# A new order for the loading phase of a fused attention and gated feed-forward kernel, with x of batch 0 loaded as fp32 and every batch's x read by column-tiled matmuls

## The chip, the cores and the metric

The kernel runs on one core of a Trainium2 chip. A core has a matmul engine (TensorE; its matmuls are PE in the profile, its weight loads PEld), a vector engine (VectorE, DVE), a scalar engine for activations (ScalarE, ACT), a general engine (GpSimd, POOL) and an engine that issues transfers (SyncE, SP). Each has its own instruction queue, executed in order. They meet through semaphores, in a large on-chip memory (SBUF) and in the accumulators of the matmul engine (PSUM). [...]

The metric is the device time of one execution in microseconds. Before the change three runs gave a median of 223.96 us (223.51 to 224.49).

## The reference

There are 8 batches with 8 heads each. A batch has 512 tokens x and 32 state rows, of width 64 per head.

```python
scores = scale * x @ state.T          # (512, 32) per head
a = softmax(scores)                   # over the 32 state rows
xread = a @ state                     # (512, 64)
scores2 = scale * state @ x.T         # the same scores, transposed
a2 = softmax(scores2)                 # over the 512 tokens
sread = a2 @ x                        # (32, 64)
x = concatenate([xread, sread], axis=2)   # heads side by side: 544 rows of 512 per batch
gate = 1 / (1 + exp(-(x @ w_gate)))   # (rows, 1536)
out = (gate * (x @ w_val)) @ w_out    # (rows, 512)
```

In all, 4352 rows of 512 numbers are written. All inputs and the output are fp32.

## The kernel before

Matmuls run in bf16. For the rows that come from tokens, a @ state @ w is computed as a @ (state @ w): `sw_visit` and `sw_wide` multiply the state of a batch with column ranges of `wg` and `wv` and leave the products in PSUM, `sw_cp` copies them to the tile `SW`, and `gv_mm(b, f)` multiplies `SW` with the transposed a (`aT`) for the 128 columns of slice f. `gv_th` (ACT) and `gv_glu` (DVE) form the gated product; the sigmoid is a tanh, with the factor 0.5 put on the output. `out_mm(b, k)` multiplies four slices with `wo`; the output of one row group is complete after three such calls, is copied by ACT and sent out.

For a, `xT_mm` and `xT_cp` (or transposing DMAs on SP, `at_xT_dma`) transpose x, `S_mm` makes scores, `S_exp` exponentials, `n_sum` or `n_sums` and `n_mul` or `n_muls` normalise over the state rows, and `aT_mm` with `aT_cp` (or transposing DMAs, `aT_dma`) transposes the result. `at_Eb` makes a bf16 copy of the exponentials on POOL.

The second softmax needs, for each state row, a sum over tokens of exponential times x (the read of x) and the sum of the exponentials. Before the change there are two ways. For batches 0 to 2, `sr_mm` makes 16 matmuls with x as the stationary side (L265), and the sums either with eight matmuls against `ones` (batch 0, L262) or with one matmul of sums that POOL has folded (`p_tok`, `p_fold`, `n_add`; L257); `sr_fin` divides (L270, L278) into the tile `XS`. For batches 3 to 7, `rd_mm` makes 32 column-tiled matmuls (L292): 32 columns of exponentials are the stationary side, so that four of them use four quarters of the array; the moving side is a copy of x with a column of ones (`xs`, made by `cast_xs`), so that the sum comes as column 65. `rd_fin` divides and `rd_dma` transposes into `XS` by a DMA on SP. `XS` is used for the 256 state rows at the end.

The order of the work is written out by hand: each engine executes its instructions in the order of the calls. PSUM has four pools: `GV` with two banks, `OU` and `AT` with one, `SWP` with four. Batches 0 and 1 are computed call by call (L477 to L731), together with all loads of weights; from L734 a loop goes over batches 2 to 8, where 8 stands for the state rows, with one slice of batch b, one part of the output of b - 1 and some preparation of b + 1 in each step.

Loads in the first phase: x of batch 0 comes half as fp32 on SP with casts on three engines (L478, L491, `cast_xp`) and half by POOL's queue with conversion (`load_xh`, L483); x of batch 1 and all weights come by POOL's queue (`load_xh`, `load_w`, `load_wo`), and so does the state of batches 2 to 7 (`load_sb`). POOL issues a load when it reaches it, behind its own work. `warm(n, place)` issues n matmuls of 512 columns whose result is not read.

Of the kernel before, what the change touches and what calls it, by code (L numbers as in the profile page):

```python
# [8 lines left out]
FP = mybir.dt.float32  # L9
# [7 lines left out]
def kernel(  # L17
# [36 lines left out]
    ones = wp.tile((128, 2, 128), BF, name="ones")  # L54
# [130 lines left out]
    def n_add(b):  # L185

        E2 = ap_.tile((128, 2, 2, 4, Ns), FP, name="E2", bufs=1)
        held["E4", b] = ap_.tile((128, 2, 4, Ns), FP, name="E4")
        nc.vector.tensor_tensor(E2, E1s[b][:, 0:2], E1s[b][:, 2:4], ALU.add)
        nc.vector.tensor_tensor(held["E4", b], E2[:, 0], E2[:, 1], ALU.add)  # L190

    def p_fold(b):

        E4, add = held["E4", b].rearrange("p e j n -> p e (j n)"), nc.gpsimd.tensor_tensor
        F, G = (ap_.tile((128, 2, 4 * Ns), FP, name=n, bufs=1) for n in ("F", "G"))
        half = [slice(e * 64, e * 64 + 64) for e in range(2)]
        for e in range(2):
            pool(F[half[e], 0], E4[half[1 - e], e])
        for e in range(2):
            add(G[half[e], 0], E4[half[e], e], F[half[e], 0], ALU.add)  # L200
        for q in range(4):
            r = q ^ 1
            pool(F[32 * q:32 * q + 32, 1], G[32 * r:32 * r + 32, 0])
        add(G[:, 1], G[:, 0], F[:, 1], ALU.add)
        hl = held["hl", b] = ap_.tile((128, 4 * Ns), BF, name="hl")
        pool(hl, G[:, 1])
        for e in range(2):
            lo = slice(e * 64 + 32, e * 64 + 64)
            add(hl[lo], G[lo, 1], hl[lo], ALU.subtract)

    def p_tok(b):

        add = nc.gpsimd.tensor_tensor
        E5 = ap_.tile((128, 2, 4, Ns), FP, name="P1", bufs=1)
        E4 = held["E4", b] = ap_.tile((128, 2, 4, Ns), FP, name="E4")
        add(E4, E1s[b][:, 0], E1s[b][:, 1], ALU.add)
        add(E5, E1s[b][:, 2], E1s[b][:, 3], ALU.add)
        add(E4, E4, E5, ALU.add)

# [27 lines left out]
    def sr_parts(b):  # L247
        ps = held["sr", b]
        return (ps[:, 0:256].rearrange("p (j e n) -> p j e n", j=4, e=2),
                ps[:, 256:384].rearrange("p (j n) -> p j n", j=4))  # L250

    def sr_mm(b, place):
        Eb = Ebs[b]
        held["sr", b] = place[0].tile((128, 512), FP, name="srp", tag=place[1])
        sr, sm = sr_parts(b)
        if ("hl", b) in held:
            nc.tensor.matmul(sm, pick, held["hl", b], start=True, stop=True)  # L257
            terms = []
        else:
            terms = [(e, Eb[:, c, e]) for e in range(2) for c in range(4)]  # L260
        for i, (e, rhs) in enumerate(terms):
            nc.tensor.matmul(sm, ones[:, e], rhs, start=(i == 0), stop=(i == len(terms) - 1))  # L262
        for j in range(4):
            for c in range(4):
                nc.tensor.matmul(sr[:, j], xbs[b][:, c, 2 * j:2 * j + 2].rearrange("p h d -> p (h d)"),  # L265
                                 Eb[:, c, :, j], start=(c == 0), stop=(c == 3))

    def sr_inv(b):
        r2 = held["r2", b] = ap_.tile((128, 4, Ns), FP, name="r2")
        nc.vector.reciprocal(r2, sr_parts(b)[1])  # L270

    def sr_fin(b):
        if ("r2", b) not in held:
            sr_inv(b)
        sr, r2 = sr_parts(b)[0], held["r2", b]
        for e in range(2):
            rows = slice(e * 64, (e + 1) * 64)
            nc.vector.tensor_tensor(XS[rows, b], sr[rows, :, e], r2[rows], ALU.mult)  # L278

# [3 lines left out]
    def rd_mm(b):  # L285

        ps = AT[0].tile((128, 512), FP, name="rdp", tag=AT[1])
        rd = held["rd", b] = ps[:, :2 * D + 2].rearrange("p (e d) -> p e d", e=2)
        for e in range(2):
            for c in range(4):  # L290
                for j in range(4):
                    nc.tensor.matmul(rd[j * Ns:(j + 1) * Ns, e], Ebs[b][:, c, e, j], xs[:, c, 2 * j + e, :D + 1],  # L292
                                     start=(c == 0), stop=(c == 3))

    def rd_fin(b):
        rd = held["rd", b]
        r2 = ap_.tile((128, 2, 1), FP, name="rr")
        nc.vector.reciprocal(r2, rd[:, :, D:])
        xr = held["xr", b] = ap_.tile((128, 2, D), BF, name="xr")
        nc.vector.tensor_tensor(xr, rd[:, :, :D], r2.to_broadcast((128, 2, D)), ALU.mult)  # L300
# [84 lines left out]
    def out_mm(b, k, place=None):  # L385
# [10 lines left out]
        if f0 == 8:  # L396
            res = fp.tile((128, 512), FP, name="res", bufs=4)
            nc.scalar.activation(res, ops[b, c], AF.Copy, scale=0.5)  # L398
            if b < B:
                n = 256 if 4 * (B - 1) - 4 <= 4 * b + c < 4 * (B - 1) else 512  # L400
# [25 lines left out]
    def warm(n, place):  # L426

        ps = place[0].tile((128, 512), FP, name="warm", tag=place[1])
        for _ in range(n):
            nc.tensor.matmul(ps.rearrange("p (r k) -> p r k", r=4), ones[:, 0], ones[:, 0].unsqueeze(1).to_broadcast((128, 4, 128)), start=True, stop=True)  # L430
# [44 lines left out]
    pick = wp.tile((128, 128), BF, name="pick")  # L475
    pre = wp.tile((128, 2), FP, name="pre")
    make_identity(nc, ident)  # L477
    load_xp(0, nc.sync, 0, 2)  # L478
    for e in range(2):
        nc.vector.memset(ones[:, e, e * 64:e * 64 + 64], 1.0)  # L480
        nc.vector.memset(ones[:, e, 64 - e * 64:128 - e * 64], 0.0)
    warm(1, SWP)
    load_xh(0, 4, 4)  # L483
    warm(2, GV)
    warm(2, AT)
    load_s(0, nc.scalar)
    cast_s(0, vec)
    load_xh(1, 4, 4)
    warm(2, GV)
    warm(4, SWP)  # L490
    load_xp(0, nc.sync, 2, 2)  # L491
    cast_xp(0, act, 2, 2)
    zero(sbz, vec)
    sT_mm(0, SWP)
    xT_mm(0, 1, SWP)
    cast_xp(0, pool, 0, 2)
    cast_x(0, vec, 0, 2)
    zero(sTd, vec)
    xT_mm(0, 0, SWP)
    sT_pad(1, vec)  # L500
    xT_cp(0, 0, act)
    sT_pad(0, act)
    xT_mm(0, 3, SWP)
    S_mm(0, 0, SWP, (0,))
    load_xh(1, 0, 4)
    xT_mm(0, 2, GV)
    load_sb(1)
    xT_cp(0, 1, vec)
    S_mm(0, 0, AT, (1,))
    load_w(1, 256, 256)  # L510
    S_exp(0, 0)
    cast_x(0, vec, 6, 2)
    xT_mm(1, 2, SWP, 2)
    xT_cp(0, 2, vec)
    xT_cp(0, 3, act)
    S_mm(0, 1, GV, (0,))
    S_mm(0, 1, AT, (1,))
    warm(1, GV)
    n_sum(0, 0)
    S_exp(0, 1)  # L520
    cast_x(0, act, 2, 2)
    load_w(0, 256, 256)
    xT_mm(1, 0, GV, 2)
    xT_cp(1, 0, act, 2)
    load_w(0, 1024, 512)
    xT_cp(1, 2, vec, 2)
    S_mm(1, 1, OU)
    S_mm(1, 0, SWP)
    n_sum(0, 1)
    load_w(1, 1024, 512)  # L530
    sT_mm(1, SWP)
    n_mul(0, 1, vec)
    S_exp(1, 1)
    cast_x(0, vec, 4, 2)
    n_mul(0, 0, pool)
    at_Eb(0)
    aT_mm(0, AT)
    S_exp(1, 0)
    load_w(1, 0, 256)
    sT_cp(1, act)  # L540
    sw_visit(0, 256, 256)
    sr_mm(0, OU)
    sw_visit(1, 256, 256)
    n_sums(1)
    n_muls(1, vec)
    load_w(0, 0, 256)
    aT_cp(0, 0, act)
    sw_cp(0, 256, 2, 0, act)
    sw_cp(0, 256, 2, 1, act)
    aT_cp(0, 1, act)  # L550
    gv_mm(0, 2, GV)
    load_sb(2)
    sw_cp(1, 256, 2, 1, vec)
    gv_th(0, 2)
    sw_cp(1, 256, 2, 0, act)
    aT_mm(1, AT)
    gv_glu(0, 2)
    aT_cp(1, None, act)
    sw_visit(1, 1024, 512, 0)
    sw_visit(0, 1024, 512, 0)  # L560
    gv_mm(0, 3, GV)
    sw_cp(1, 1024, 0, 0, vec)
    sw_cp(1, 1024, 0, 1, vec)
    gv_th(0, 3)
    sw_cp(0, 1024, 0, 0, vec)
    gv_glu(0, 3)
    sw_cp(0, 1024, 0, 1, act)
    sw_visit(1, 1024, 512, 1)
    sw_cp(1, 1024, 1, 1, act)
    load_x(2, nc.gpsimd)  # L570
    sw_cp(1, 1024, 1, 0, vec)
    sw_visit(0, 1024, 512, 1)
    sw_cp(0, 1024, 1, 0, act)
    gv_mm(1, 2, GV)
    gv_th(1, 2)
    sw_cp(0, 1024, 1, 1, vec)
    cast_x(1, pool, 0, 2)
    gv_mm(1, 8, SWP)
    zero(sTz, vec)
    load_w(0, 512, 512)  # L580
    gv_glu(1, 2)
    gv_th(1, 8)
    at_Eb(1)
    gv_mm(0, 11, SWP)
    gv_mm(1, 3, GV)
    gv_th(0, 11)
    gv_glu(1, 8)
    cast_x(1, pool, 4, 2)
    load_w(1, 512, 512)
    gv_th(1, 3)  # L590
    gv_glu(0, 11)
    gv_glu(1, 3)
    gv_mm(0, 8, SWP)
    gv_th(0, 8)
    gv_glu(0, 8)
    gv_mm(0, 10, GV)
    gv_th(0, 10)
    sw_visit(0, 0, 256)
    sw_cp(0, 0, 2, 1, act)
    gv_glu(0, 10)  # L600
    sw_cp(0, 0, 2, 0, act)
    sw_visit(1, 0, 256)
    sw_cp(1, 0, 2, 0, vec)
    sT_mm(2, AT)
    gv_mm(0, 9, GV)
    gv_mm(1, 9, SWP)
    gv_th(0, 9)
    sw_cp(1, 0, 2, 1, act)
    load_sb(3)
    gv_th(1, 9)  # L610
    cast_x(2, vec, 0, 4)
    gv_mm(1, 11, SWP)
    gv_glu(0, 9)
    gv_glu(1, 9)
    gv_mm(1, 0, GV)
    sw_visit(0, 512, 512, 0)
    zero(pick, pool)
    gv_th(1, 11)
    gv_glu(1, 11)
    cast_x(2, pool, 4, 4)  # L620
# [196 lines left out]
```

## Time and profile before

| what | value |
|---|---|
| median of three runs | 223.96 us (223.51 to 224.49) |
| profiled execution: its time, its span | 224.5 us, 222.7 us |
| PE busy | 213.9 us (96%) |
| DVE, ACT, POOL busy | 123.5, 129.2, 66.6 us |
| first matmul of x of batch 0's second half | 8.12 us |
| first gate matmul (`gv_mm`) | 16.64 us |
| first state product of the loop over batches | 56.38 us |
| DMA traffic | 26.75 MB, mean 120 GB/s |

The profile is of one execution; times in it are microseconds from the start of its span. A busy engine is one with an instruction in flight. The matmuls of one core overlap, so the busy time of a group can be less than the number of matmuls by the duration of one. "L394" is a line of the kernel. In the chain of waits the profile goes back from the last instruction to what released it, step by step, so the chain shows which engine's work set the time at each moment. A line of the timeline gives start, length, engine, line, operation, tiles with shapes and the number of instructions merged into it, and in brackets the idle time before with what ended it.

### The profile page before, as it was taken

The page shows a single profiled execution, that of the slowest core. Times are in us where ns is not written, and L with a number is a line of the kernel's source. Part 1 is how long each engine was busy: PE and PEld are TensorE (multiplying, and loading weights), DVE is VectorE, ACT ScalarE, POOL GpSimd, SP SyncE. Part 2 cuts the span into 40 slices and gives each one's busy share as a digit, 9 for nine tenths or more (in the row PEclk, how much of TensorE's full clock was granted, in tenths as well). Part 3 has the DMA queues.
Part 4 walks back from the last instruction along what each step waited for, and adds up shares of the span by engine and source line. Part 5 has one row for each costly group of instructions (what it writes and reads, how often), then busy time and mean ns, then how long its engine had stood idle before and what let it go on. Part 6 is the DMA issues. An engine that isn't in the chain of part 4 may idle for free.

```text
span 222.7 us, 4790 instructions
## 1 busy us (share of the span) xinstructions
PE 213.9 (96%) x1839; PEld 107.4 (48%) x1862; DVE 123.5 (55%) x214; ACT 129.2 (58%) x243; POOL 66.6 (30%) x124
## 2 busy tenths in 40 slices
PE   8679999999999999999999999999999999999994
PEld 3554444544444444444444444444444444466744
DVE  3599989986467445744484448354754334422301
ACT  3398797627675667656674866666756444433311
POOL 6699498556341036001800072003200000000001
PEclk9799999999999999999999999999999999999999
DMA  6999996984598349924552206421122111211114
GB/s 152 158 202 248 244 177 106 151 224 132 134 260 260 61 74 281 199 47 142 169 149 69 101 0 97 130 70 45 47 74 77 49 50 53 66 69 49 50 29 113
DMA packets 40982, 26.75 MB, mean 120 GB/s; under 512 B 23456, under 2 KB 36768, under 8 KB 40960
## 3 DMA queue, kind: packets, MB, share of 16 engines
q1 hardware_dynamic: 31088, 18.33, 31.6%
q0 software_dynamic: 9584, 7.93, 21.1%
q8 instruction: 14, 0.23, 0.4%
q10 hardware_dynamic: 288, 0.20, 0.3%
q14 instruction: 8, 0.07, 0.1%
HBM read 18.35 MB, written 8.91 MB: 122 GB/s over the span
## 4 chain that ended last, share of the span: by engine, by line
PE 90%; ACT 3%; DMA 3%; DVE 1%; issue 1%; POOL 0%; POOLq 0%
PE outp L394 38%; PE gvp L363 37%; PE swp L311 5%; PE gvp L366 5%; DMA xf<-in_x_dram 3%; PE Sp L152 1%; PE outp L416 1%; ACT E L157 1%; DVE SW L349 1%; PE rdp L292 1%; ACT xT L134 1%; PE xTp L131 0%; ACT aT L241 0%; ACT SW L349 0%; PE srp L265 0%
## 5 line engine op out<-in xcount | busy, mean ns | idle before, releaser
L378 DVE SCALAR_TENSOR_TENSOR glu<-th,gvp 128x512 bf16<-128x512 f32 (+1 forms) x108 | 70.1, 656 | 79.0 <-ACT th L373 63.5
L394 PE MATMUL outp<-wo,glu 128*128 128x512 bf16 x373 | 95.9, 379 | 1.3 <-issue 0.2
L363 PE MATMUL gvp<-aT,SW 128*128 128x512 bf16 x384 | 96.5, 379 | 0.5 <-ACT aT L241 0.5
L373 ACT ACTIVATE th<-gvp 128x512 f32<-128x512 f32 (+1 forms) x108 | 61.9, 576 | 59.3 <-PE gvp L363 45.8
L394 PEld LDWEIGHTS <-glu 128*128 128x128 bf16 x396 | 37.8, 98 | 41.9 <-issue 0.4
L363 PEld LDWEIGHTS <-SW 128*128 128x128 bf16 x384 | 36.2, 98 | 45.1 <-issue 4.2
L349 ACT CAST SW<-swp 128x512 bf16<-128x512 f32 x70 | 39.0, 586 | 4.3 <-PE swp L311 3.5
L398 ACT ACTIVATE res<-outp 128x512 f32<-128x512 f32 x33 | 19.7, 597 | 17.7 <-PE outp L394 17.7
L103 POOL COPY pre<-th 128x1 f32<-128x1 f32 x5 | 0.9, 188 | 69.0 <-ACT th L373 69.0
L407 POOL DMA_DIRECT2D out_dram<-res x2 | 1.1, 537 | 59.7 <-ACT res L398 59.7
L349 DVE CAST SW<-swp 128x512 bf16<-128x512 f32 x26 | 17.2, 684 | 2.9 <-PE swp L311 2.9
L163 POOL CAST Eb<-E 128x256 bf16<-128x256 f32 x32 | 12.0, 418 | 10.9 <-ACT E L157 10.9
L115 POOL CAST xb<-xf 128x1024 bf16<-128x1024 f32 x11 | 11.2, 1041 | 4.0 <-DMA xf<-in_x_dram 3.2
L157 ACT ACTIVATE E<-Sp 128x512 f32<-128x512 f32 x16 | 9.6, 604 | 3.3 <-PE Sp L150 2.8
L283 POOL CAST xs<-xf 128x1024 bf16<-128x1024 f32 x10 | 10.2, 1044 | 0.0
L311 PE MATMUL swp<-wg,sTc 64*32 64x512 bf16 (+1 forms) x192 | 8.7, 327 | 0.0
L170 DVE TENSOR_REDUCE rs<-E 128x16 f32<-128x512 f32 x12 | 8.2, 680 | 0.5 <-ACT E L157 0.4
L224 DVE TENSOR_TENSOR ab<-E,ri 128x512 bf16<-128x512 f32 x11 | 8.2, 742 | 0.0
L311 PE MATMUL swp<-wv,sTc 64*32 64x512 bf16 (+1 forms) x192 | 7.5, 322 | 0.0
L311 PEld LDWEIGHTS <-sTc 64*32 64x32 bf16 x384 | 4.9, 91 | 5.2 <-issue 3.0
L366 PE MATMUL gvp<-XS,wg 128*128 128x256 bf16 x48 | 7.2, 273 | 0.0
L366 PE MATMUL gvp<-XS,wv 128*128 128x256 bf16 x48 | 7.2, 273 | 0.0
(88 smaller groups left out, 129.0 us busy)
## 6 DMA issues: line engine op xcount, KB each, us to landing
out_dram<-res SPq DMA_DIRECT2D x27, 256.0 KB, 3.2
xf<-in_x_dram SPq DMA_DIRECT2D x4, 1024.0 KB, 6.6
xf<-in_x_dram POOLq DMA_DIRECT2D x2, 1024.0 KB, 7.5
wo<-in_moe_w_out_dram POOLq DMA_DIRECT2D x3, 512.0 KB, 5.6
out_dram<-res SPq DMA_DIRECT2D x9, 128.0 KB, 1.9
wg<-in_moe_w_gate_dram POOLq DMA_DIRECT2D x2, 512.0 KB, 9.3
wv<-in_moe_w_val_dram POOLq DMA_DIRECT2D x2, 512.0 KB, 10.4
xf<-in_x_dram POOLq DMA_DIRECT2D x3, 256.0 KB, 6.6
```

Of the source, the lines that this page charges most:

```text
L115: cp(xbs[b].rearrange("p c h d -> p h c d")[:, lo:lo + n], (xhs if b in xhs else xfs)[b][:, lo:lo + n])
L157: nc.scalar.activation(E1s[b][:, :, :, 2 * i:2 * i + 2].rearrange("p c e j n -> p (c e) j n"), held["S", b, i].rearrange("p c e j n -> p ( ...
L163: nc.gpsimd.tensor_copy(Ebs[b][:, c], E1s[b][:, c])
L283: pool(xs.rearrange("p c h d -> p h c d")[:, lo:lo + n, :, :D], xfs[b][:, lo:lo + n])
L311: nc.tensor.matmul(pss[e][j * Ns:(j + 1) * Ns, o:o + n], sTc[rows, b, j] if b > 1 else sTd[rows, b, 2 * j + e, e], (wg, wv)[w][rows, j, lo ...
L349: cp(*sw_left.pop((b, lo, w, e)))
L363: nc.tensor.matmul(ps, SWs[b][:, g, w, fs], aTs[b][:, :, g], start=(g == 0), stop=(g == 1))
L366: nc.tensor.matmul(ps, (wg, wv)[w][:, j, fs], XS[:, :, j], start=(j == 0), stop=(j == 3))
L373: nc.scalar.activation(th, held["gv", b, f][0], AF.Tanh, scale=0.5)
L378: nc.vector.scalar_tensor_tensor(glus[b][:, f], held["th", b, f], 1.0, held["gv", b, f][1], ALU.add, ALU.mult)
L394: nc.tensor.matmul(ops[b, c], glus[b][:, f, c * 128:(c + 1) * 128], wo[:, f], start=(f == 0), stop=(f == NF - 1))
L398: nc.scalar.activation(res, ops[b, c], AF.Copy, scale=0.5)
```

## The change

It has three parts. x of batch 0 comes wholly as fp32 on SP's queue, in four pieces, and is cast by DVE (three pieces) and ACT (one). All batches use `rd_mm`: batches 0 to 2 read x from the tiles that are there anyway (`xhs`, `xbs`), and their sums come from further column-tiled matmuls of one column against `ones`; the old path (`sr_*`, `p_fold`, `p_tok`, `n_add`, `pick`) is gone, and the three new results are transposed into `XS` by DMAs in the loop, at batch 2, slice 8. The calls of the loading phase stand in a new order, with unread matmuls in more places; all weights stand before x of batch 2 in POOL's queue, the tile `sTd` is zeroed by POOL at the start, `sTz` by POOL later. The output is sent in halves for three more row groups.

```diff
+    ones = wp.tile((128, 1), BF, name="ones")
+    wm = wp.tile((128, 128), BF, name="wm")
...
-    def rd_mm(b):
+    def rd_mm(b, place):
...
             for c in range(4):
                 for j in range(4):
-                    nc.tensor.matmul(rd[j * Ns:(j + 1) * Ns, e], Ebs[b][:, c, e, j], xs[:, c, 2 * j + e, :D + 1],
-                                     start=(c == 0), stop=(c == 3))
+                    h, o, Eb = 2 * j + e, rd[j * Ns:(j + 1) * Ns, e], Ebs[b][:, c, e, j]
+                    if b > 2:
+                        nc.tensor.matmul(o, Eb, xs[:, c, h, :D + 1], start=(c == 0), stop=(c == 3))
+                    else:
+                        xh = xhs[b][:, h, c] if b in xhs else xbs[b][:, c, h]
+                        nc.tensor.matmul(o[:, :D], Eb, xh, start=(c == 0), stop=(c == 3))
+            if b < 3:
+                for c in range(4):
+                    for j in range(4):
+                        nc.tensor.matmul(rd[j * Ns:(j + 1) * Ns, e, D:], Ebs[b][:, c, e, j], ones, start=(c == 0), stop=(c == 3))
...
-                n = 256 if 4 * (B - 1) - 4 <= 4 * b + c < 4 * (B - 1) else 512
+                n = 256 if 4 * (B - 1) - 7 <= 4 * b + c < 4 * (B - 1) else 512
...
-    make_identity(nc, ident)
-    load_xp(0, nc.sync, 0, 2)
...
-    load_xh(0, 4, 4)
...
-    load_xp(0, nc.sync, 2, 2)
...
+    zero(sTd, pool)
+    load_xp(0, nc.sync, 4, 2)
+    nc.vector.memset(wm, 0.0)
+    warm(1, GV)
+    make_identity(nc, ident)
+    warm(1, OU)
+    warm(1, OU)
+    warm(2, GV)
+    warm(1, AT)
+    warm(1, GV)
+    load_s(0, nc.scalar)
+    load_xp(0, nc.sync, 2, 2)
+    cast_xp(0, vec, 4, 2)
+    load_xh(1, 4, 4)
...
+    load_xh(1, 0, 4)
+    load_xp(0, nc.sync, 6, 2)
+    warm(2, GV)
+    cast_xp(0, vec, 6, 2)
+    load_xp(0, nc.sync, 0, 2)
+    warm(1, SWP)
+    sT_mm(0, SWP)
+    cast_xp(0, vec, 0, 2)
+    xT_mm(0, 2, AT)
...
+    load_w(0, 256, 256)
+    load_w(1, 256, 256)
...
+    S_mm(0, 1, AT, (1,))
+    warm(4, GV)
+    S_exp(0, 1)
+    xT_mm(1, 2, AT, 2)
...
+    load_w(0, 1024, 512)
+    load_w(1, 1024, 512)
+    n_mul(0, 0, pool)
+    load_w(1, 512, 512)
+    aT_mm(0, OU)
+    at_Eb(0)
...
+    rd_mm(0, OU)
+    at_Eb(1)
+    n_sums(1)
+    sw_cp(1, 256, 2, 0, act)
+    nc.gpsimd.memset(xs[:, :, :, D:], 1.0)
+    gv_mm(0, 2, SWP)
+    gv_mm(0, 3, GV)
...
+    load_sb(1)
+    load_w(1, 0, 256)
...
+    load_sb(2)
...
+    rd_mm(1, GV)
+    sw_visit(0, 1024, 512, 1)
+    sw_cp(0, 1024, 0, 1, vec)
+    load_w(0, 512, 512)
+    sw_visit(1, 1024, 512, 1)
+    sw_cp(0, 1024, 1, 0, act)
+    rd_fin(1)
+    sw_cp(0, 1024, 1, 1, vec)
+    load_sb(3)
+    gv_mm(0, 8, GV)
+    gv_mm(0, 11, SWP)
...
+    load_w(0, 0, 256)
...
+    load_x(2, nc.gpsimd)
+    gv_mm(0, 10, GV)
+    load_wo(2)
...
+    sT_mm(1, AT)
+    sT_cp(1, act)
+    sw_visit(1, 512, 512, 0)
...
+    load_wo(0)
...
+    cast_x(2, pool, 0, 4)
+    sw_cp(1, 512, 1, 1, act)
+    sw_visit(0, 0, 256)
+    load_wo(1)
...
+    out_mm(0, 7, OU)
+    sT_cp(3, vec)
+    zero(sTz, pool)
+    pad(2, 6)
+    gv_glu(0, 7)
+    at_xT_dma(2)
...
+    load_x(3, nc.gpsimd)
+    out_mm(0, 4)
+    out_mm(0, 9)
+    S_mm(2, 0, GV)
+    cast_x(3, pool, 4, 4)
+    S_exp(2, 0)
+    S_mm(2, 1, GV)
+    S_exp(2, 1)
+    gv_glu(1, 7)
+    n_sums(2)
+    out_mm(0, 11)
+    gv_mm(1, 10, GV)
+    n_muls(2, vec)
...
+    aT_dma(2)
...
+    at_xT_dma(3)
...
+    rd_mm(2, SWP)
...
     for b in range(2, B + 1):
...
-                    rd_mm(nb)
+                    rd_mm(nb, AT)
...
                     rd_dma(nb)
+                if b == 2 and f == 8:
+                    for q in range(3):
+                        rd_dma(q)
```

440 lines of the change are left out of this document (145 added, 295 removed).

## The prediction

> **What bounds the kernel now.** I read the page first (busy shares, the slices), then the chain of waits in order of time, then the busy time per microsecond, then the timeline where the change acts. The page:
>
> ```profile
> span 222.7 us, 4790 instructions
> PE 213.9 (96%) x1839; PEld 107.4 (48%) x1862; DVE 123.5 (55%) x214; ACT 129.2 (58%) x243; POOL 66.6 (30%) x124
> PE   8679999999999999999999999999999999999994
> DMA  6999996984598349924552206421122111211114
> PE 90%; ACT 3%; DMA 3%; DVE 1%; issue 1%; POOL 0%; POOLq 0%
> ```
>
> PE is full from about 20 us to the end; only the first four slices (5.57 us each) have room, and there the DMA engines are full as well. The chain in order of time (start, length, what) shows where PE takes over:
>
> ```profile
> 1.47 6.61 DMA xf<-in_x_dram
> 8.12 0.61 PE xTp L131 x4
> 9.62 0.60 ACT E L157
> 11.18 0.60 ACT E L157
> 16.64 0.61 PE gvp L363 x2
> 20.46 0.45 PE swp L311 x8
> 20.91 5.34 PE gvp L363 x24
> ...
> 56.38 0.77 PE swp L311 x32
> 57.15 0.97 PE gvp L363 x4
> ```
>
> Up to 20.9 us other things end last: a POOL load of half of x of batch 0 (lands 8.08), exponentials, copies. From 20.9 every long piece is PE. The loop over batches starts at 56.38. The change leaves the loop's PE work alone, so the end moves with that start. Two stretches of the busy time (PE, PEld, DVE, ACT, POOL, clock, DMA share, GB/s) and four lines of the timeline carry the rest:
>
> ```profile
> 7.00:8.00 1.00, 0.00 (x0) 0.00 (x0) 0.00 (x0) 0.32 (x1) 1.00 (x2) 1.00 1.28 168
> 8.00:9.00 1.00, 0.88 (x11) 0.88 (x12) 0.45 (x1) 0.00 (x0) 1.00 (x2) 0.50 1.20 135
> ```
>
> ```profile
> 19.70 0.27 PEld L311 LDWEIGHTS <-sTd 64*32 64x32 bf16 x9 [0.42 <-DMA wv<-in_moe_w_val_dram]
> 23.19 3.06 DVE L378 SCALAR_TENSOR_TENSOR glu<-th,gvp 128x512 bf16<-128x512 f32 x5
> 53.69 5.13 SPq L139 DMA_TRANSPOSE xT<-xb  x4
> 68.02 0.42 PE L292 MATMUL rdp<-xs,Eb 128*32 128x65 bf16 x32
> ```
>
> The reader is to see: PE has nothing to do from 7 to 8 and its clock is then halved; the last early wait is for weights (19.70); back to back, a glu costs DVE 0.61 us; four transposing DMAs hold SP's queue 5.1 us; a whole column-tiled read is 32 matmuls started within 0.35 us (its follower starts at 68.37).
>
> **The change part by part.** All is set against the profiled execution: span 222.7, its own time 224.5. The median of the runs, 223.96, is 1.26 above this span, and I keep that.
>
> 1. *x of batch 0 on SP.* Now two 256 KB pieces on SP land at 4.14 (issued 0.74, 3.4 to landing) and 4.85 (when ACT's cast starts), so 0.7 us a piece; pieces three and four then land at 5.55 and 6.3. If POOL's loads take half of the engines they come at 6.3 and 7.7. I take 6.3, because POOL's first load starts 0.95 us later than before (the zeroing of sTd, 1024 columns, moves to POOL ahead of the identity; POOL's own 64- and 128-column memsets of 0.163 and 0.205 us give 0.66 to 0.8 ns a column); range 5.9 to 7.7, against 8.08. The fourth cast goes to DVE (half of its 0.825 us cast of 1024 columns, 0.41; at most ACT's 0.62).
>
> 2. *The chain to the first gate matmul.* From 6.3: cast 0.41, four transposes and their result 0.45, copy 0.42, a second copy and the score matmuls 0.7: E of the first half starts at about 8.3 (now 9.62) and of the second at 8.9 to 9.1 (now 11.18). Sums and reciprocals 2 x (0.69 + 0.25), product 0.75: a^T can be transposed at 11.5 (now 13.80). Then the weights rule: wg columns 256 to 511 land at 13.9 now (6.92 + 7.0). The state of batches 2 and 3, which lies ahead of them in POOL's queue and lands 0.5 us after x, moves behind, and the extra SP load moves 0.13 MB earlier, 0.35 us at the 363 GB/s of the third microsecond: about 13.05. Two visits of 0.28 and two ACT copies of 0.6 give a first gate matmul at 14.7, against 16.64.
>
> 3. *Where PE stays full.* The next limit is wv columns 1024 to 1535. It lands at 19.6 now (8.38 + 11.2) and by the same two terms at 18.75 after. The visit that reads it, its result and the slower copy (DVE 0.68) put the next gate matmul at 19.85, against 20.84 now. Both kernels have done the same by then (two gate matmuls, all visits of columns 256 and 1024), except the read of batch 1 (now later) and the transposes of state 2, 3 (now earlier). Gain 0.99 us; 0 if the weights do not come earlier; 1.5 at most, where ACT and DVE alone (three early visits' copies, two tanh, products) reach 19.35.
>
> 4. *The reads.* Removed from the full part: the reads of batches 1 and 2, each 0.06 + 0.47 on the chain, 1.06. Added there: one new read and the transposes of state 2, 3 (0.23). A new read is 64 matmuls: 32 of 64 columns, 0.35 by the row at 68.02, and 32 of one column that no row shows: between 0 and 0.35, since they are issued like the 65-column ones. I take 0.35, as issue is what they share with that row. 1.06 - 0.70 - 0.23 is -0.13; bounds -0.48 and 0. The two reads in the loading phase lie in waits for weights and copies; without that cover they would cost 0.7 each.
>
> 5. *DVE, ACT, POOL between 20 and 56 us.* DVE loses casts of x (2.1), the three old finishes (1.54 each, now 0.45), n_add (1.1) and sTz (0.91); POOL loses both folds (7.2 and 4.5 us). DVE gains copies of a^T (1.5) and casts (1.2). No net term: PE has at most 1 us of idle there to win. In the new order DVE has some 13 glus and copies in a row between 22.4 and 31; at 0.61 to 0.64 they fit the 8.8 us of PE's seven gates and seven small visits, at the lone 0.685 they would not, and PE would lose 0.4 to 0.8. I take 0, since such runs come back to back in this trace.
>
> 6. *Later weights.* All weights now go before x of batch 2. At 2.6 us per 1 MB (13.9 to 16.5 for one) the second half of wv lands at 21.4 and of wg at 26.3; PE wants them at 22.5 and 26.5. The rows of wo follow at 33 to 39, wanted at 38 to 41. Cost 0, but the cover of wg is 0.2 us: each microsecond that this stream is late is one that PE waits.
>
> 7. *SP's queue.* x of batch 2 lands near 31 (now 25.4), its transposing DMAs run 34 to 39; batch 2's scores are placed near 43. From there: exponentials 1.6, sums 1.6, products 1.3, a^T's four transposes 5.1, then xT of batch 3 behind them 5.2 and 1.2 to land: 16.1 us. PE has 16.6 us of work from these scores to batch 3's. Cost 0, cover 0.5. The three added XS transposes (1.18 each, 3.5 in all) stand near 83 us before the load of batch 6, the transposes of batch 5 and a^T of batch 4; the last ends at about 99.4 instead of 98.3 and is read at 103.8. The six further half-size output issues (0.5 each) are waited for by nobody. Cost 0.
>
> Sum: -0.99 - 0.13 = -1.1: loop start 55.3, span 221.6, time 222.85.
>
> *The clock.* The granted clock was 0.50 from 8 to 11 us, after PE had stood still from 6.2 to 8.1. In the new order PE's longest gap between 5 and 9 us is about 0.6 by the steps above, so I take a full clock; whether that is busy enough, no row shows. [...]
>
> **The rivals.** *Weights no earlier.* The DMA share is 1.2 to 1.4 through this phase, so the stream may be set by bytes alone: wv at 19.6, PE full at 20.8. Against: fewer bytes lie ahead of it. Time 223.8. *The clock falls again.* Four unread 512-column matmuls then take 0.43 each instead of 0.22 and stand ahead of batch 1's transposes; with these 1 us is lost there, 0.6 after the weights' wait: 223.5. *More is won:* the weights arrive at 17.8, ACT and DVE set 19.35, and half of the 1 us of idle between 20.8 and 56.4 goes: 221.9. *Slower: the transposing DMAs.* Batch 3's xT stands behind batch 2's a^T on SP. PE waits as soon as that chain takes over 16.6 us, and the kernel is slower by over 0.5% from 2.2 us later still. For it: landing of these transposes is 2.5 us in the median, but 5.4 and 4.0 at the longest, and four have taken 6.30; together 2.9 + 1.6 + 1.1 = 5.6 us, of which 0.5 is covered: at worst 227.9, and at half of it 225.2. Against: by 48 us the weights are all loaded, and now too this chain ends (60.0) only 0.3 us before its use.
>
> **How the numbers follow.** A measurement of this kernel tells 0.5% (1.1 us) from no change, so the edges are 222.84 and 225.08. Forecast (222.2 to 223.5 by terms 3 and 4): 0.55, half on each side of the edge. More won 0.14, weights no earlier 0.08, clock 0.07, slower 0.16. Faster 0.275 + 0.14 = 0.42, same 0.275 + 0.15 = 0.42, slower 0.16. The range leaves out the lower part of "more won" and most of the slower case: 221.6 to 225.4.
>
> **What would show it.** Steps 1 and 2: transposes of batch 0 done by 7.1, E at 8.3 and 9.0, first gate matmul near 14.7. Step 3: the visit of wv column 1024 starts at 18.8 and PE is full from 19.9. Step 4: new reads of 0.7 us. Step 6: no wait of PE for wg near 26.5. Step 7: batch 3's scores start without a wait for xT. The loop's first visit at 55.3 and the same 166.3 us from there. Wrong if PE idles between 20 and 56 us for DVE or for a weight, or if the gate matmuls start at 14.7 but PE is full no sooner than now.

## The result and the profile after

The changed kernel took 225.25 us in the median of 16 runs, the kernel before 223.92 in 16 runs beside them: a ratio of 1.0058 (95% interval 1.004 to 1.0076). It is slower by 0.6%, where 222.85 us was forecast. Runs more than 1.5% above the fastest of their kernel are left out of this ratio and of all below. The page of the changed kernel:

```profile
span 224.3 us, 5054 instructions
PE 216.3 (96%) x2001; PEld 106.6 (48%) x2001; DVE 117.3 (52%) x204; ACT 128.6 (57%) x241; POOL 56.3 (25%) x92
PE   8788999999899999999999999999999999999994
PE 84%; SPq 6%; DMA 5%; ACT 1%; issue 1%; DVE 1%
```

The chain of waits of the same execution, in order of time (start, length, what):

```profile
2.26 5.20 DMA xf<-in_x_dram
...
14.60 0.97 ACT SW L288 x2
15.62 1.68 PE gvp L302 x7
...
18.54 0.82 issue
...
20.97 2.75 PE gvp L302 x12
...
53.98 1.91 SPq L140
...
58.55 3.12 DMA xT<-xb
```

And its waits (engine, line, released by: us in total, times, longest):

```profile
PE Sp L153 <- DMA xT<-xb: 1.3, 2, 0.9
PE swp L250 <- issue: 0.8, 1, 0.8
```

Two things are new. SP's queue, which the chain before does not name, now holds 6% of it, and DMA has gone from 3 to 5%: PE waits for xT of batch 3 at that batch's scores, at 61 us, and a little for xT of batch 4 at 85 us. And PE stands still for 0.82 us at 18.54 us in the middle of eight matmuls of one state product, without waiting for anything that the profile shows ("issue"). The gate matmuls do start earlier (15.18 us, 16.64 before), but PE is full from 20.97 (20.91 before), and the loop's first state product starts where it did (56.32, timeline; 56.31 before).

A second profiled execution of each kernel changes the picture of the start. This is the kernel before again, its chain and two microseconds of its busy time (PE, PEld, DVE, ACT, POOL, clock, DMA share, GB/s):

```profile
16.13 0.61 PE gvp L363 x2
...
20.40 5.34 PE gvp L363 x24
...
55.86 0.78 PE swp L311 x32
```

```profile
7.00:8.00 1.00, 0.00 (x0) 0.00 (x0) 0.00 (x0) 0.28 (x1) 1.00 (x2) 1.00 1.14 137
8.00:9.00 1.00, 0.71 (x16) 0.72 (x16) 0.29 (x1) 0.00 (x0) 1.00 (x2) 1.00 1.31 166
```

PE has the same hole as in the first execution, but the granted clock stays at 1.00, PE is full 0.51 us earlier and the span is 222.3, not 222.7. This is the ordinary case: 25 of 28 runs of the kernel before in one session lie between 223.4 and 224.1 at a mean clock of 0.998 or more, and the three at 0.992, the mean clock of the first profiled execution, took 224.8 to 225.0. Set side by side, the second executions (first row from the chain, the others from the timeline):

| point | before | changed | difference |
|---|---|---|---|
| PE full (gate matmuls without a break) | 20.40 | 19.92 | -0.48 |
| first state product of the loop | 55.80 | 55.81 | +0.01 |
| first half of batch 3's scores done | 60.43 | 61.45 | +1.02 |
| span | 222.3 | 223.2 | +0.9 |

So between these two executions half a microsecond is won at the start, given back between 20 and 56 us, and a whole one is lost at batch 3's scores. In two of the 16 runs of the changed kernel the mean clock was lower (0.992 and 0.985, at 226.49 and 232.06 us); in the others it was 0.999 or more, so the loss of the median is not the clock's. The experiments took these three places apart.

### The profile page after: what moved, and what is told of

Its sections match the earlier page's. It is cut to its first block, busy times and chain, and to the rows that moved or that the text cites. A ratio compares the mean times of both kernels' runs of the same rounds, so it can differ in the third digit from the quotient of the medians.

```text
span 224.3 us, 5054 instructions
## 1 busy us (share of the span) xinstructions
PE 216.3 (96%) x2001; PEld 106.6 (48%) x2001; DVE 117.3 (52%) x204; ACT 128.6 (57%) x241; POOL 56.3 (25%) x92
## 4 chain that ended last, share of the span: by engine, by line
PE 84%; SPq 6%; DMA 5%; ACT 1%; issue 1%; DVE 1%
PE outp L333 34%; PE gvp L302 34%; PE swp L250 5%; PE gvp L305 5%; SPq L140 4%; DMA xT<-xb 2%; DMA xf<-in_x_dram 2%; SPq L211 2%; PE Sp L153 1%; PE outp L355 1%; PE rdp L225 1%; PE Sp L151 1%; SPq L83 1%; PE warm L369 1%; PE aTp L197 1%
## 5 line engine op out<-in xcount | busy, mean ns | idle before, releaser
L333 PE MATMUL outp<-wo,glu 128*128 128x512 bf16 x396 | 98.2, 379 | 0.0
L288 ACT CAST SW<-swp 128x512 bf16<-128x512 f32 x73 | 40.6, 586 | 7.6 <-PE swp L250 6.9
L116 POOL CAST xb<-xf 128x1024 bf16<-128x1024 f32 x12 | 12.3, 1042 | 15.9 <-DMA xf<-in_x_dram 15.9
L288 DVE CAST SW<-swp 128x512 bf16<-128x512 f32 x23 | 15.4, 684 | 1.3 <-PE swp L250 1.3
L164 POOL CAST Eb<-E 128x256 bf16<-128x256 f32 x32 | 12.5, 433 | 10.5 <-ACT E L158 10.4
L369 PE MATMUL warm<-wm 128*128 128x512 bf16 x17 | 6.6, 523 | 1.0 <-DVE wm L417 1.0
## 6 DMA issues: line engine op xcount, KB each, us to landing
wo<-in_moe_w_out_dram POOLq DMA_DIRECT2D x3, 512.0 KB, 11.4
```

Of the source, the lines that this page charges most:

```text
L116: cp(xbs[b].rearrange("p c h d -> p h c d")[:, lo:lo + n], (xhs if b in xhs else xfs)[b][:, lo:lo + n])
L164: nc.gpsimd.tensor_copy(Ebs[b][:, c], E1s[b][:, c])
L288: cp(*sw_left.pop((b, lo, w, e)))
L333: nc.tensor.matmul(ops[b, c], glus[b][:, f, c * 128:(c + 1) * 128], wo[:, f], start=(f == 0), stop=(f == NF - 1))
```

## The experiments

Kernels of one session share the runs of the kernel before, whose median was 223.7 to 223.9 us in all of them.

**The kernel before once more.** Here and below "theory" and a letter stand for an explanation that the text put on record ahead of the run gives, "rival" for another.

> The kernel before itself, for a second profiled execution of it. The first one had a granted clock of 0.50 from 8 to 11 us and a span of 222.7; its other executions had a full clock and a median span of 222.0. If the clock's fall is what made the first one long (theory K), this one has a full clock throughout, its first gate matmul and its full stretch come 0.4 to 0.8 us earlier, the loop starts at 55.6 to 55.9 and runs 166.3 us from there. If the first one was ordinary (rival), the loop starts at 56.4 again.

Measured: ratio to itself 0.9987 (0.9961 to 1.0013), and the profile above: full clock, PE full at 20.40, loop start 55.80. Theory K holds, for this pair of executions: the one that the forecast was worked out on was one whose clock had fallen.

**The changed kernel once more.**

> The changed kernel itself once more, beside the kernels it is compared with. Ratio to the kernel before 1.004 to 1.009; a gap of 0.4 to 0.9 us without a wait in the visit of wg column 1024 near 18.5 us, and a wait of PE of about 1 us for xT at batch 3's first scores.

Measured: ratio 1.0069 (1.0055 to 1.0084), a gap of 0.35 us (0.4 to 0.9 expected), a wait of 0.83 us at batch 3's scores. Besides these, PE waited 0.52 us at 48.93 us for a DVE copy, which the first execution did not show.

**x of batch 3 ahead of a^T of batch 2 on SP's queue.**

```diff
+    load_x(3, nc.gpsimd)          # behind load_wo(1)
...
     out_mm(0, 2)
-    load_x(3, nc.gpsimd)
+    cast_x(3, pool, 4, 4)
+    cast_x(3, pool, 0, 4)
+    at_xT_dma(3)
...
-    cast_x(3, pool, 4, 4)
...
-    cast_x(3, pool, 0, 4)
...
-    at_xT_dma(3)
```

> The load of x of batch 3, its casts and its four transposing DMAs are moved ahead of batch 2's scores, so that SP's queue takes them before a^T of batch 2; nothing else changes. Theory A (SP's queue: xT of batch 3 behind a^T of batch 2 is late by 1.1 us, and a smaller wait at batch 4's scores follows from it): both waits are gone, from the loop's first visit to the end 1.6 us are saved, span 222.7, ratio to the kernel before 1.000 (0.997 to 1.002). Rival B (the loss lies in the loop for another reason, contention or the SP queue's total load): the wait moves to a^T of batch 2 or stays at batch 4, span 224 or more, ratio 1.005. Should x of batch 3 in front of the other loads push the rows of wo, a wait of PE at the first output matmuls (38 to 41 us) would show.

Measured: ratio 1.011 (1.0078 to 1.0142), span 224.7. The waits at batches 3 and 4 are gone, and from the loop's first state product (58.33) to the end it takes 166.4 us, as in the kernel before: for the loop, theory A. But the loop starts 2 us late, because PE waits 2.1 us for xT of batch 2 (the transposing DMAs of x up to 46 us: issues, and us from issue to landing, least, median, most):

```profile
L140 SPq DMA_TRANSPOSE xT<-xb x5: 1190/1282/4132, 33.6 to 45.1; - x5
DMA to landing us min/median/max: 2.4/8.7/9.7
```

In the changed kernel the four DMAs of batch 2 landed 5.3 us after their issue in the median (6.0 in its second execution); with 1 MB of x of batch 3 in transfer beside them, the five here, one of them of batch 3, took 8.7, and one issue held the queue for 4.1 us. The expectation had looked for a price at the rows of `wo`; it was paid here.

**Column sums over the whole array.**

```diff
-                    for j in range(4):
-                        nc.tensor.matmul(rd[j * Ns:(j + 1) * Ns, e, D:], Ebs[b][:, c, e, j], ones, start=(c == 0), stop=(c == 3))
+                    nc.tensor.matmul(rd[:, e, D:], Ebs[b][:, c, e].rearrange("p j n -> p (j n)"), ones, start=(c == 0), stop=(c == 3))
```

> In the new reads, the column sums of E go as 8 one-column matmuls over the whole array instead of 32 on column tiles: the same numbers, 48 PE instructions (24 matmuls and their weight loads) fewer in each read. Theory F (the 0.82 us in which PE stands still without a wait at 18.54 us is PE's instruction stream arriving late, so it sits at a place in the count of PE's instructions, about 445 after the start): the gap moves to an instruction 48 places later in the kernel, into the read of batch 1, or vanishes behind the wait for wv; PE is full earlier by up to 0.8 us, loop start 55.4 to 56.0. Rival W (the gap belongs to that visit, its PSUM tile or a wait that the trace does not name): it stays at the sixth matmul of the visit of wg column 1024 with 0.8 us. Both expect the reads to get shorter by 0.1 to 0.3 us each, and the wait at batch 3's scores to stay. Ratio to the kernel before: F 1.000 to 1.004, W 1.004 to 1.006.

The weight loads around the gap, in the changed kernel (first two lines) and in this one:

```profile
18.12 0.12 PEld L250 LDWEIGHTS <-sTd 64*32 64x32 bf16 x6
19.36 0.09 PEld L250 LDWEIGHTS <-sTd 64*32 64x32 bf16 x2 [1.12 <-issue]
```

```profile
18.30 0.10 PEld L228 LDWEIGHTS <-Eb 128*32 128x32 bf16 x2
18.57 0.17 PEld L228 LDWEIGHTS <-Eb 128*32 128x32 bf16 x14 [0.17 <-issue]
```

The first read has 24 pairs of weight load and matmul fewer. The break was behind the sixth of the visit's second eight weight loads; it is now behind the visit's last two, 16 and 4 of the second read, and two more: 24 loads later, in another operation on another tile. So it sits at a place in PE's instruction stream (theory F), not in that visit. PE is full at 19.54 and the loop starts at 55.38. Yet the ratio is 1.0068 (1.0056 to 1.0081), above what either theory gave: the waits at batches 3 and 4 grew to 1.30 and 0.31 us. Both theories missed on another point: the reads got longer, 0.82 us on the chain for batch 2's, 0.59 with the tiled sums.

The traces say more about the gap. Wherever it is seen it stands behind PE's 223rd weight load. Between 3 and 21 us each trace has one packet of 16 KB on the DMA queue named "instruction". It ends at 17.91 us in the first execution of the changed kernel and at 17.01 in the second, and in the 15 profiled executions of the changed kernel and its variants between 16.80 and 19.53; in all 15 PE's 224th weight load starts 1.30 to 1.56 us after that end, with a gap where PE was there sooner and without one where it was not. In the kernel before it starts 6.4 us after it, and there is no gap. This is strong support for theory F; no run moved that packet alone.

**Both edits.**

> Both edits together: x of batch 3 early and column sums over the whole array. If A and F both hold the gains add: span 221.9 to 222.4 and ratio 0.996 to 0.998. If A alone holds, ratio 1.000 or 0.999; if neither, 1.004 to 1.006.

Neither: ratio 1.0134 (1.0097 to 1.0172). With xT of batch 3 first on SP, it is a^T of batch 2 that comes too late:

```profile
57.87 1.02 PE L301 MATMUL gvp<-aT,SW 128*128 128x512 bf16 x4 [1.33 <-DMA aT<-ab]
```

In either order one of the two groups of four DMAs came late.

**Half of x of batch 0 by POOL's queue.**

```diff
+    load_xh(0, 4, 4)
+    load_xp(0, nc.sync, 2, 2)
     zero(sTd, pool)
-    load_xp(0, nc.sync, 4, 2)
...
-    load_xp(0, nc.sync, 2, 2)
-    cast_xp(0, vec, 4, 2)
...
-    load_xp(0, nc.sync, 6, 2)
...
-    cast_xp(0, vec, 6, 2)
```

> The new order, but half of x of batch 0 comes by POOL's queue as 2-byte numbers as before, and the other half in two pieces by SP. Theory C (the gate matmuls and PE's full stretch hang on the arrival of the weights and on the gap without a wait, not on x of batch 0): E of batch 0 is up to 0.5 us later, the loop's start stays within 0.3 us of 56.4, ratio to the kernel before 1.004 to 1.008. Rival D (all that is gained early comes from x of batch 0 on SP): x lands near 8.1 again, loop start 57.0 or later, ratio 1.008 to 1.012.

```profile
6.57 1.07 PE L132 MATMUL xTp<-ident,xf 128*128 128x128 bf16 x16 [1.24 <-DMA xf<-in_x_dram]
...
46.04 0.55 PE L153 MATMUL Sp<-sTz,xT 128*128 128x64 bf16 x13 [2.13 <-DMA xT<-xb]
```

The timeline shows all x of batch 0 transposed by 7.6 us (8.5 in the changed kernel's first execution) and PE full at 19.76: the early start does not hang on SP carrying all of x, and rival D falls. Theory C is half right: what follows in POOL's queue comes later, PE waits 0.46 us for wg near 27 us and 2.13 for xT of batch 2, the loop starts at 58.2, ratio 1.013 (1.0093 to 1.0168), beyond what either theory gave. The chain to the first gate matmul hangs here on a load of x of batch 1 (it lands at 11.02).

**No unread matmuls.** All `warm` calls are left out; nothing that the output needs goes.

> All unread matmuls of the loading phase are left out (17 matmuls, so 34 PE instructions with their weight loads). Theory F (the gap without a wait sits at a fixed place in PE's instruction stream): the gap moves 17 pairs of weight load and matmul later, from behind the sixth weight load of the visit of wg column 1024 to behind the fifteenth of the first sixteen 64-column matmuls of batch 1's read. On the clock: theory G (the unread matmuls keep the clock full between 5 and 11 us): without them the granted clock drops to 0.5 somewhere between 6 and 12 us, the first gate matmul comes 0.3 to 1 us later; rival H: the clock stays full and nothing moves but the gap. The wait at batch 3's scores stays in both.

Measured: ratio 1.0116 (1.0089 to 1.0143), against 1.0069 for the changed kernel in the same session: they are worth 0.5%. The four transposes of one group of heads took 0.61 us instead of 0.40, as they did at a clock of 0.50 in the first execution of the kernel before (8.12 us), and the first gate matmul came at 17.26 (14.60), yet the clock's record shows 1.00 up to 14 us. On the record theory G missed, on the slower start it was right; why the two disagree is open. PE came to the gap's place only at 20.76 us and there was no gap. The profiled execution, 229.9 us where the other five took 225.5 to 227.4, shows the clock later: PE waited 2.65 us for xT of batch 2 up to 48.06, and then the clock fell (columns as above):

```profile
47.00:48.00 1.00, 0.00 (x0) 0.00 (x0) 0.00 (x0) 0.00 (x0) 0.00 (x0) 1.00 1.04 295
48.00:49.00 1.00, 0.94 (x15) 0.59 (x16) 0.00 (x0) 0.52 (x2) 0.31 (x1) 0.87 0.64 229
49.00:50.00 1.00, 1.00 (x4) 0.43 (x3) 0.40 (x1) 0.56 (x2) 1.00 (x2) 0.50 0.10 16
51.00:52.00 1.00, 1.00 (x10) 0.15 (x16) 0.90 (x2) 0.56 (x1) 1.00 (x2) 0.50 0.40 156
```

Here a long wait was paid twice, the second time by 3.4 us at half clock.

**a^T of batch 2 on PE.**

```diff
-    aT_dma(2)
...
     gv_glu(1, 10)
+    aT_mm(2, GV)
+    aT_cp(2, 0, act)
     sw_cp(2, 1, 0, 0, vec)
+    aT_cp(2, 1, vec)
```

> a^T of batch 2 is made by eight transposes on PE and two copies from PSUM in place of four transposing DMAs on SP; xT of batch 3 then has SP's queue to itself once its cast is done at 51 us. Nothing else is changed. Theory A (SP's queue makes xT of batch 3 late): its DMAs run from 51.1 to 56.3 and land by 59.4, no wait at batch 3's scores, the load of x of batch 4 is issued 2 us earlier and the wait at batch 4's scores goes too; PE pays about 0.5 us for the transposes ahead of the loop; from the loop's first visit to the end 166.3 us; span 1.1 us below the changed kernel's. Rival B (xT lands late because of what the DMA engines carry): the wait stays at 0.5 us or more.

SP's queue and the chain:

```profile
50.20 5.83 SPq L140 DMA_TRANSPOSE xT<-xb  x4
```

```profile
60.31 0.23 PE Sp L153 x8
```

Both waits are gone, as theory A has it; the load of x of batch 4 is issued at 57.30 (60.86). PE pays 0.45 us for the transposes. Span 222.6 against 223.2: 0.6 won, not 1.1; the ratio, 1.006 (1.0035 to 1.0084), does not tell this from the changed kernel. With whole-array sums as well:

> a^T of batch 2 on PE and the column sums of the new reads by 8 matmuls over the whole array. If A and F both hold, the gains add: PE full from 19.5, loop start 55.9, 166.3 us from there, span 222.2 against 222.0 of the kernel before in the last session: ratio 0.998 to 1.002. If only A holds: 1.002 to 1.004.

1.0045 (1.0028 to 1.0063): outside both ranges, lower than the changed kernel by a quarter of a per cent, with intervals that overlap.

**The scores of batches 3 and 4 asked for later.**

```diff
+        d = int(nb in (3, 4))
...
-                if f in (1, 2):
-                    S_mm(nb, f - 1, AT)
+                if f in (1 + d, 2 + d):
+                    S_mm(nb, f - 1 - d, AT)
...
-                if f in (2, 3):
+                if f in (2 + d, 3 + d):
...
-                elif f == 4:
+                elif f == 4 + d:
...
-                if f == 3:
+                if f == 3 + d:
```

> The scores of batches 3 and 4 (and their exponentials, sums, products and bf16 copies) stand one gate step later in the loop, 1.73 us; queues, transfers and PE's work stay as they are. Theory A (xT of batch 3 is late by up to 1.3 us against the place where PE asks for it): no wait at batch 3's scores, none at batch 4's, from the loop's first visit to the end 166.4 us, span 0.8 to 1.3 us below the changed kernel's 223.2, ratio to the kernel before 1.001 to 1.003. Rival (asking later only moves the wait: xT comes later still, or a^T of batch 3 is then late): span as the changed kernel's, ratio 1.005 to 1.008.

Measured: 1.0041 (1.002 to 1.0063), where the changed kernel had 1.0069 in another session; this lies between the two theories. The profiled execution still has a wait of 1.04 us at batch 3: its xT landed at 63.6, because the product of batch 2 on DVE took 1.91 us, the first of xT's issues 2.41, and the last landed 4.5 us after its issue. How late this chain is varies between executions by more than the 1.73 us given.

> The later scores and the column sums by 8 matmuls over the whole array. If A and F hold, the loop starts at 55.4 and runs 166.4 us: span 221.8, ratio to the kernel before 0.998 to 1.000. If the loop's wait stays, 1.005.

1.0032 (1.0001 to 1.0063). No wait is left in the loop, but the profiled execution had half clock from about 10.3 to 13.7 us, after PE waited 1.11 us for the last piece of x of batch 0; its loop starts at 58.03. Of the twelve executions seven had a mean clock of 0.992 or less.

**POOL's casts behind DVE's product.** The 0.5 us wait for a DVE copy led here. The changed kernel's second execution, DVE, POOL and PE:

```profile
46.43 1.85 DVE L183 TENSOR_TENSOR ab<-E,ri 128x1024 bf16<-128x1024 f32 x1
```

```profile
46.16 1.04 POOL L116 CAST xb<-xf 128x1024 bf16<-128x1024 f32 x1 [6.09 <-DMA xf<-in_x_dram]
47.14 2.43 POOL L164 CAST Eb<-E 128x256 bf16<-128x256 f32 x4
```

```profile
48.93 0.41 PE L250 MATMUL swp<-wv,sTc 64*32 64x512 bf16 x8 [0.52 <-DVE SW L288]
```

The product takes 1.22 us in the kernel before, where POOL copies and casts nothing beside it. Here a cast runs until 47.2, and 47.2 + 1.22 is 48.4, about where the product ends; then POOL's four copies take 2.43 us instead of 1.43 (in the kernel before, and in the run below). In four executions the excess of the product follows what was left of the cast when it began; the product ends 0.14 or 0.15 us before the cast's end and 1.22 us together:

| kernel | product starts | cast ends | cast's end and 1.22 | product ends |
|---|---|---|---|---|
| changed, first | 47.48 | 47.71 | 48.93 | 48.78 |
| changed, second | 46.43 | 47.20 | 48.42 | 48.28 |
| a^T on PE | 46.42 | 46.81 | 48.03 | 47.89 |
| scores later | 46.94 | 47.77 | 48.99 | 48.85 |

```diff
-    cast_x(3, pool, 4, 4)
...
     n_muls(2, vec)
+    at_Eb(2)
+    gate(abs_[2][:, 0, 0, 0:1])
+    cast_x(3, pool, 4, 4)
+    cast_x(3, pool, 0, 4)
...
-    at_Eb(2)
-    cast_x(3, pool, 0, 4)
```

> POOL makes the bf16 copies of batch 2's E first, then waits for DVE's product of batch 2 and only then casts x of batch 3; all else as in the changed kernel, whose product took 1.85 us (1.22 in the kernel before) where it met POOL's cast, after which PE waited 0.5 us for the DVE copy behind it. Theory P (the DVE product, with two inputs in SBUF, stands still until POOL's cast of 1.04 us ends): the product takes 1.22 us, PE's wait of 0.5 us for a DVE copy of SW near 49 us is gone, a^T's DMAs on SP start 0.6 us earlier and so does xT of batch 3: the wait at batch 3's scores shrinks from 0.8 to 0.2 to 0.5 us; span 0.3 to 0.8 us lower, ratio to the kernel before 1.002 to 1.005. Rival (the product is long for another reason): it stays at 1.3 to 1.9 us, ratio 1.006 or more.

```profile
46.70 1.23 DVE L183 TENSOR_TENSOR ab<-E,ri 128x1024 bf16<-128x1024 f32 x1
```

```profile
45.09 1.43 POOL L164 CAST Eb<-E 128x256 bf16<-128x256 f32 x4 [4.75 <-ACT E L158]
```

Theory P: both are at their own length again and PE's wait there is gone; ratio 1.004 (1.0018 to 1.0063). But the wait at batch 3's scores stayed at 0.85, not 0.2 to 0.5, as xT's DMAs again took 6.02 us, and the span, 223.5, was not below the changed kernel's 223.2. Why the first of xT's four issues takes 1.9 to 2.4 us in these kernels and the others 1.26 is open. That the product is longer beside a cast is measured (up to 1.91 us, 1.23 without one); what holds it up is not shown.

**All three causes undone.** Whole-array sums, later scores and the casts behind the product; then with three more unread matmuls (`warm(3, SWP)` behind `xT_mm(0, 3, GV)`); then with whole-array sums in batch 0's read alone.

> The casts after the product, the column sums over the whole array and the later scores of batches 3 and 4, together. If A, F and P hold: loop start 55.1 to 55.4, 166.4 us from there, span 221.5 to 221.8, ratio 0.996 to 0.999 where the clock is full; where the clock falls early (theory K: the last piece of x of batch 0 lands late and PE thins out from 7 to 10 us) 1.5 to 3 us more.

> As the one before, with three more unread 512-column matmuls behind the third group of x transposes of batch 0, where PE waits for the last piece of x. If PE's thin stretch from 7 to 10 us is what makes the clock fall, no execution of this kernel has a lower mean clock than 0.998, and the spread of its times is 1 us or less; ratio 0.996 to 1.000. If the clock falls for another reason, the spread stays as in the kernel without them.

> As the kernel with all three causes undone and the three more unread matmuls, but only the read of batch 0 sums over the whole array; batches 1 and 2 go back to one-column matmuls on column tiles. Theory M (a change between column tiles and the whole array costs PE: the read of batch 2 took 0.82 us with whole-array sums and 0.59 with tiled ones): the read of batch 2 takes 0.59 us again, PE's gap without a wait stays near 18.5 us at a place 24 pairs of weight load and matmul later than in the changed kernel and is 0 to 0.3 us long; loop start 55.0, span 221.4 to 221.6, ratio to the kernel before 0.997 to 0.999. Rival (the gap comes back with its full 0.35 to 0.8 us, since PE reaches the place earlier): ratio 0.999 to 1.001.

| kernel | ratio to the kernel before | loop start | span |
|---|---|---|---|
| changed | 1.0069 (1.0055 to 1.0084) | 55.81 | 223.2 |
| all three undone | 1.0003 (0.9974 to 1.0033) | 54.96 | 221.7 |
| and unread matmuls | 0.9994 (0.9975 to 1.0013) | 55.31 | 221.7 |
| and tiled sums for batches 1, 2 | 0.9988 (0.9963 to 1.0013) | 54.70 | 221.1 |

The chain of the last one:

```profile
18.19 0.12 issue
...
19.35 2.82 PE gvp L305 x12
...
54.77 0.77 PE swp L253 x32
```

With the three causes undone the loss is gone; how it divides among them the ratios of the single edits do not resolve. The last kernel's gap of 0.12 us stands behind PE's 223rd weight load again: by its place in the program that is 21 loads later than in the changed kernel, 24 for the shorter read less the three unread matmuls put in ahead of it (the expectation forgot those three). The loop start is 1.1 us below the kernel before, but the medians (223.42, and 223.71 beside it) and the interval do not show a faster kernel. On the clock the expectation failed: with the three more unread matmuls one of twelve executions still had a mean clock of 0.993, and of the last kernel two (0.992 and 0.985). How often the clock falls varied between sessions: the kernel with later scores and whole-array sums, seven of twelve, issues the same work up to 40 us as the one with all three undone, two of twelve. What makes it fall is open.

## Why the prediction was wrong, step by step

The step that failed is step 7, which gave SP's chain to xT of batch 3 a cost of 0: PE waited 0.8 to 1.3 us for it. Two more terms failed, step 5's "no net term" (0.5 us) and the base of step 3's saving (0.5 us). The second execution's span, 223.2, is 1.6 above the 221.6 forecast: 0.5 of it lies ahead of the loop's start (55.81, forecast 55.3), where PE waited 0.52 for a DVE copy, and 1.1 behind it (167.4 instead of 166.3), where PE waited 0.83 for xT.

- *The base.* "The median of the runs, 223.96, is 1.26 above this span, and I keep that." Here 0.5 us was lost before any step. The profiled execution's own time is 1.8 above its span; the median is nearer only because the median execution is shorter: full clock, PE full at 20.40. The prediction saw the clock at 0.50 and gave it a rival for the kernel after, but never asked what the kernel before does without it.
- *Steps 1 and 2.* The last piece of x landed at 7.46, not 6.3 (range 5.9 to 7.7): three pieces came 0.7 us apart as forecast, the fourth 5.2 us after its issue. E came at 9.54 and 10.17 (8.3 and 9.0 forecast), the first gate matmul at 15.18 in the first and 14.60 in the second execution (14.7). In the second execution that piece of x landed at 6.88, and both followed 0.58 us earlier. "Then the weights rule" did not hold: in both executions the chain runs from this landing through E and ACT's copies to the first gate matmul, and PE waited for no weight. That 14.60 agrees with 14.7 is luck; the terms given for it add up to 14.8.
- *Step 3, "Gain 0.99 us".* Against the full-clock execution of the kernel before 0.48, with a gap of 0.35 us in it. The time forecast, 19.85, was met by the second execution (19.92), but by luck: it was worked out from the landing of wv of column 1024, which came at 19.0 in the first execution and 18.1 in the second, while PE reached that visit at 20.28 and 19.22. What set it was the chain from x of batch 0 and the gap. No term stood for the gap: the new reads were costed by time on PE, not by their 128 PE instructions each, of which the first read's stand ahead of it. In the variants with unread matmuls and a full clock, a gap of 0.12 us or less let PE be full at 19.35 to 19.9. The row at 19.70 on which the step rests shows a weight load that waits; PE itself was busy with gate matmuls up to there, and the chain of the kernel before goes through three copies on DVE, a row that the prediction's excerpt leaves out:

```profile
18.59 1.83 DVE SW L349 x3
```

- *Step 4.* Right in the main. A new read is 0.59 to 0.62 us (0.7 taken), and the work from PE full to the loop is 35.35 us against 35.40 in the first executions, -0.05 where -0.13 was forecast.
- *Step 5, "No net term".* Wrong: in the second execution the product of batch 2 meets POOL's cast and PE waits 0.52 us for a DVE copy behind it (0.58 with the later scores); in the first it met only the cast's end and PE did not wait. PE idle for DVE between 20 and 56 us was one of the signs that the prediction itself named. The step counted DVE's and POOL's work separately. The run of glus and copies that it doubted, 22 to 31 us, held: 0.64 to 0.71 us each, and PE did not wait.
- *Step 6.* Right: no wait for a weight. That its cover is thin shows where half of x went by POOL: 0.46 us of waiting for wg.
- *Step 7, "Cost 0, cover 0.5".* From batch 2's scores to xT of batch 3 it forecast 16.1 us against 16.6 us of PE work. The second execution took 17.8 (43.27 to 61.08): the product 1.85 instead of 1.3, xT's four issues 6.17 instead of 5.2, the rest in small pieces; PE asked after 16.8. The wait is 0.8 to 1.3 us, with 0.3 to 0.4 more at batch 4 in some executions. The three added XS transposes and the smaller output issues were waited for by nobody, as said.
- *The clock* stayed full in both profiled executions of the changed kernel, as taken.
- *The rivals.* "Slower: the transposing DMAs" names the wait that came, with a chance of 0.16; that its "half of it 225.2" agrees with 225.25 is luck, since the wait for a DVE copy and the base are in the measured time. Against it stood that "now too this chain ends (60.0) only 0.3 us before its use"; but there the chain hung on POOL's cast and not on SP, so it told nothing of the new one. "Weights no earlier" did not occur. "The clock falls again" did not in the two profiled executions, but in two of the 16 runs (0.992 and 0.985).

## What to carry to other kernels

Look at the granted clock of the profiled execution before taking savings from it: if it fell there and the median did not see that, what a change saves there is not saved in the median. Read a wait from the engine that the chain runs through: a weight load that waits is not a matmul that waits. A chain of queue steps with 0.5 us of cover needs the longest durations in the trace, not the median ones, and every step in it has to be asked what runs on the neighbouring engine at that time. A gain at the start only reaches the end when the next wait in the program has at least as much slack.

## What the runs showed of the hardware

- PE's break without a wait sits at a fixed place in its instruction stream: behind 223 weight loads in every trace that shows it. It was up to 0.82 us long and ended between 18.2 and 19.4 us. In 15 executions the 224th weight load started 1.30 to 1.56 us after the end of the only packet of 16 KB on the queue named "instruction" at that time, which took 0.9 us. That instructions arriving late cause the break is argued from this; no run varied the packet by itself. The changed kernel's page counts 15 packets on that queue, 0.25 MB.
- Eight one-column matmuls over the whole array between tiled ones cost more than 32 tiled ones: 0.82 against 0.59 us for the read of batch 2.
- A DVE product of 1.22 us (two inputs, 128x1024) took up to 1.91 us beside a cast on POOL, and four copies on POOL beside it 2.43 us instead of 1.43.
- In one kernel the transposing DMAs took longer beside a further load of 1 MB: 8.7 us to landing in the median, against 5.3 and 6.0 without it.
- The granted clock fell from 1.00 to 0.50 after an idle PE of 1.9 us (6.2 to 8.1) in one execution of the kernel before; after 2.1 us at the same place it did not in the other. It did not after 2.13 us with half of x by POOL's queue; it did after 2.65 without unread matmuls, and after 1.11 with later scores and whole-array sums, in a stretch where PE was busy for 35 to 50% of the time (7 to 10 us). Each of the three falls lasted 3.4 us (8.0 to 11.4, 48.7 to 52.2 and 10.3 to 13.7). In these five executions the length of the idle time alone does not decide whether the clock falls.
